# The load of v moved behind the loads of the stored spectrum in SyncE's order

## The chip, the cores and the metric

The kernel runs on one core of one Trainium2 chip. The metric is the device time of one execution in microseconds (us). A profiled execution has a time of its own; the trace of it covers its span, from the first instruction of the program to the last.

## The reference, cut to what matters

A long convolution with gating (batch 4, length 12608, 128 channels), followed by a top-128 selection and a small expert layer:

```python
h_mlp  = np.maximum(pos_emb @ w1, 0.0) @ w2
h_filt = h_mlp * np.exp(-0.01 * pos)[:, None]
u  = x * v
L  = 2 * S
Uf = np.fft.rfft(u, n=L, axis=1)
Hf = np.fft.rfft(h_filt, n=L, axis=0)
y  = np.fft.irfft(Uf * Hf[None, :, :], n=L, axis=1)[:, :S, :]
a  = x * y                                   # the input of the second part
# for each batch: the 128 rows with the highest a @ w_gate
g  = 1.0 / (1.0 + np.exp(-scores[b, top_idx]))
out[b, top_idx] = a[b, top_idx] + g[:, None] * (np.maximum(xe @ w1e, 0.0) @ w2e)
```

## The kernel before

The convolution is done as real transforms of length 93 x 250, written as matmuls. The 128 channels of a batch are 32 groups of four, so there are 4 x 32 = 128 groups, and the main loop takes one group t in each step. All instructions stand on their engines in the order in which the program writes them (a manual schedule); semaphores are set by the framework.

What happens to group t, and where:

- `load_n("x", t)` and `load_n("v", t)` (line 316) bring the inputs, 250 KB each, from DRAM into rings of four (`NU`) and three (`NV`) buffers. Both are issued by SyncE (SP). In step t the loop loads x of group t + 4 and v of group t + 5 (one more in steps 0 to 3, none in step 4).
- `stage_u` (line 326) multiplies x by v on GpSimd (POOL), in step t for group t + 3. It frees a buffer of v.
- `f_s1` (line 484), the first transform on TensorE (PE), reads the product; in step t it is done for group t + 1, and it frees a buffer of x.
- `dft` (line 343), the second transform on PE, then `f_v` and `f_u` on VectorE (DVE, lines 493 and 490).
- `f_y` (lines 500 to 504, DVE) multiplies by the filter's spectrum; in step t it is done for group t - 1. In the first batch the spectrum lies in SBUF (`hh`); the loop stores it to DRAM meanwhile (`hd`, line 1309, 32 stores of 372 KB). From the second batch on `load_h` (line 332) brings it back, two loads of 186 KB a group, into a ring of three buffers. In step t it is issued for group t + 2, whose buffer is the one that `f_y` of group t - 1 has read. The last two batches keep the first three groups, so 178 such loads are issued.
- `f_sd` (lines 511 and 512, POOL), then `f_i` (line 549, PE), the inverse transform, three steps later (`LAG`), with copies on ScalarE (ACT, lines 553 and 554) and `f_c` (line 592, POOL).
- `put` (line 565) moves a part of the result within SBUF, a DMA of 126 KB on SP.

After the last group of a batch (a seam) a stage `P1` of some 40 us computes the product with x, the scores and the output: matmuls of line 639, loads of x (line 614), stores of the output (line 678). The selection of a batch runs in small pieces inside the steps of the next batch.

SP does nothing but issue DMAs, in order: an instruction that waits holds everything behind it. Besides what its data need, each DMA waits for the landing of the one eight places before it, because the framework hands out eight semaphores in turn (`DMAHW0` to `DMAHW7` in the order below).

The lines of the loop that set SP's order in a step:

```python
            if t != 4:
                load_u(t + NU + (t < 4))
...
            for k in range(4 * (t - 1) // 3, min(4 * t // 3, NG)) if t else ():
                nc.sync.dma_start(hd[:, k], hh[:, k].rearrange("p e s i -> p (e s i)"))
            load_h(t + 2)
            for k in due + [k for k in done if k % NG >= NG - 3]:
                put(k, *((JM, NJ) if k % NG >= NG - 3 else ()))
```

Of the kernel before, what the change touches and what calls it, by code (L numbers as in the profile page):

```python
# [39 lines left out]
NU, NV, NX, NH = 4, 3, 5, 3  # L40
# [198 lines left out]
def hyena_moe(ctx, tc, xg, x2, pos, bw, ww, wg, mw1, mw2, cs, c1, gx, cf, ci, wm, tk, out):  # L239
# [18 lines left out]
    def buf(name, k, shape):  # L258
        o, n, w = OFF[name]
        return view(arena, o + k % n * w, shape)  # L260
# [53 lines left out]
    def load_n(n, t):  # L314
        if t < B * NG:
            nc.sync.dma_start(buf(n, t, [NP, XC]), xg[t // NG, :, GC[t], "xv".index(n)])

    def load_u(t, e=1):
        load_n("x", t)
        load_n("v", t + e)  # L320

    def stage_u(t):
        if t >= B * NG:
            return
        x, v = buf("x", t, [NP, XC]), buf("v", t, [NP, XC])
        nc.gpsimd.tensor_tensor(out=x, in0=x, in1=v, op=ALU.mult)  # L326

    def load_h(t):
        if t < B * NG and HS[t] == "hd":
            ht = buf("ht", HI[t], [128, 2, HC])  # L330
            for e in range(2):
                nc.sync.dma_start(ht[:, e], hd[:, GC[t], e * HC:(e + 1) * HC])
# [7 lines left out]
    def dft(t, te, pq):  # L340
        for w in (1, 0):
            for a in range(0, 128, 32):
                nc.tensor.matmul(pq[w][a:a + 32], lhsT=cf_sb[:, 2 * w + a // NQ, a % NQ:a % NQ + 32],  # L343
                                 rhs=te[:, a // NQ], start=True, stop=True)
        qs = buf("qs", t, [128, HC])
        nc.scalar.copy(out=qs, in_=pq[1])  # L346
        return qs
# [130 lines left out]
    def f_s1(t, dst=None, ps=bank1):  # L478
        u = buf("x", t, [NP, 4, N3])
        te = buf("te", t, [128, 2, 4, N1]) if dst is None else dst  # L480
        tps = [view(ps[h], 0, [128, 2, 2, N1]) for h in range(2)]
        for s in range(4):
            for k, c in enumerate(BLK):
                nc.tensor.matmul(tps[s // 2][c, s % 2], lhsT=u[:, s, c], rhs=c1_sb[:, k], start=True, stop=True)  # L484
        for h in range(2):
            nc.scalar.copy(out=te[:, :, 2 * h:2 * h + 2].rearrange("p e s i -> p s e i"), in_=tps[h])  # L486
        return te.rearrange("p e s i -> p e (s i)")

    def f_u(pq, qs):
        nc.vector.tensor_tensor(out=nat(pq[0]), in0=nat(pq[0]), in1=rev(qs), op=ALU.add)  # L490

    def f_v(pq, qs):
        nc.vector.tensor_tensor(out=nat(pq[1]), in0=rev(pq[0]), in1=nat(qs), op=ALU.subtract)  # L493

    def f_y(t, uv):
        ht = buf("ht", HI[t], [128, 2, HC]) if HS[t] != "hh" else hh[:, GC[t]].rearrange("p e s i -> p e (s i)")
        mt, yz = buf("mt", t, [128, 2, HC]), buf("yz", t, [128, 2, HC])
        for e in (1, 0):
            for o, k in ((mt[:, e], 0), (uv[e], 1)):
                nc.vector.tensor_tensor(out=o, in0=uv[e], in1=ht[:, k], op=ALU.mult)  # L500
        yield yz
        nc.vector.tensor_tensor(out=yz[:, 0], in0=uv[1], in1=mt[:, 0], op=ALU.add)  # L502
        yield yz
        nc.vector.tensor_tensor(out=yz[:, 1], in0=mt[:, 1], in1=uv[0], op=ALU.subtract)  # L504
        yield yz
# [56 lines left out]
    def put(t, *cols):  # L562

        o, i = parts(t, cols or (0, NJ))
        nc.sync.dma_start(o, i)

    def turn(i):

        g, r = i % NG, i % 4
        if i > DIR:  # L570
            u = [(t, s) for t in ((i, DIR) if i == DIR + 1 else (i,)) for s in range(4)]
        elif r == 0:
            u = [(i - 1, s) for s in (1, 2, 3)] if g else []
        else:
            u = {1: [(i, 0), (i, 1), (i, 2)], 2: [(i - 1, 3), (i, 0), (i, 1)], 3: [(i - 1, 2), (i - 1, 3), (i, 0)]}[r]
            if g == NG - 1:
                u += [(i, s) for s in (1, 2, 3)]
        done = []
        for t, s in u:
            f_i(t, s)  # L580
            if s == 3:
                done.append(t)
                if t % NG >= NG - 3 and t < DIR:
                    o, i = parts(t, (0, JM))
                    nc.scalar.copy(out=o, in_=i)
        return done

    def f_c(t, ops=(ALU.subtract, ALU.add)):
        a, d = ay[:, GC[t], JM:NJ], ay[:, GC[t], NJ + JM:]
        for op in ops:  # L590
            n = NJ - JM - (op == ALU.add)
            nc.gpsimd.tensor_tensor(out=d if op == ALU.subtract else a[:, :n], in0=a[:, :n], in1=stg(t)[:, :n], op=op)  # L592
# [656 lines left out]
    def small_steps():  # L1249
        for _ in range(ND):  # L1250
            bg.hook("d")

    for t in range(NT + LAG):
        g = t % NG
        i = t - LAG
        bg.now = t
        done = turn(i) if i >= 0 else []
        if t < NT:
            pq = [bank2[2 - 2 * (t % 2) + e] for e in range(2)]
            spare[0] = [a[:, 512 - NS:] for a in bank1]  # L1260
            uv[t] = [a[:, :HC] for a in pq]
            qs = dft(t, te.pop(t), uv[t])
            if t == 0:
                rest()
            bg.hook("p", 2)
            spare[0] = [pq[0][:, HC:]]
            bg.hook("t", 1)
            spare[0] = [a[:, 512 - NS:] for a in bank1]
            bg.hook("n", 1)
            for k in ((1, 2), (3,), (4,), (5,), ())[t] if t < 5 else (t + 1,):  # L1270
                if k < NT:
                    te[k] = f_s1(k, ps=banks[6:] if k == 2 else bank1)
            spare[0] = None
            if t != 4:
                load_u(t + NU + (t < 4))
            if 0 <= t - 4 < len(fills):
                z = fills[t - 4]
                nc.scalar.activation(out=z, in_=one.to_broadcast([128, z.shape[1]]), func=AF.Copy, scale=0.0)
            o = t - 1 in uv
            if o:  # L1280
                steps = f_y(t - 1, uv.pop(t - 1))
                y = next(steps)
                next(steps)
            end = t == NT - 1
            if end:
                next(steps)
            else:
                small_steps()
            f_v(uv[t], qs)
            if o and not end:  # L1290
                next(steps)
            if not end:
                bg.hook("e")
            f_u(uv[t], qs)
            seam = i >= 0 and i % NG == NG - 1
            now = [k for k in done if seam or end or k % NG == NG - 3]
            done_ = [k for k in done if k not in now]
            for k in now:
                f_c(k)
            if o or t - 1 in ys:  # L1300
                sd[t - 1] = f_sd(t - 1, y if o else ys.pop(t - 1))
            for k in done_:
                f_c(k, (ALU.subtract,))
            if not seam and t != 4:
                stage_u(t + 3 + (t < 4))
            for k in done_:
                f_c(k, (ALU.add,))
            for k in range(4 * (t - 1) // 3, min(4 * t // 3, NG)) if t else ():
                nc.sync.dma_start(hd[:, k], hh[:, k].rearrange("p e s i -> p (e s i)"))
            load_h(t + 2)  # L1310
            for k in due + [k for k in done if k % NG >= NG - 3]:
                put(k, *((JM, NJ) if k % NG >= NG - 3 else ()))
            due = [k for k in done if k % NG < NG - 3]
            for _ in range(0 if end else NE):
                bg.hook("e")
            if i >= 0 and i % NG == NG - 1:
                *_, ys[t] = f_y(t, uv.pop(t))
            if t == NT - 1:
                sd[t] = f_last(t, uv.pop(t))
        if t >= NT:  # L1320
            for k in due:
                put(k)
            due = []
            for k in done:
                f_c(k)
        if t == NT:
            bg.drain()
            ex = Experts(picked)
        b = i // NG
        if i >= 0 and i % NG in LA[b]:  # L1330
            if i % NG == LA[b][0]:
                ph[b] = P1(b)
            k, e = divmod(LA[b].index(i % NG), 2)
            ph[b].load_a(AHEAD[k], e * HB, (e + 1) * HB)
        if i % NG == NG - 1 and i >= 0:
            bg.drain("w")
            p1 = ph.pop(b)
            p1.run(ex)
            bg.drain()
            bg = Background(topk_one(b, p1, ex))  # L1340
# [51 lines left out]
```

## Time and profile before

| | |
|---|---|
| time, median of 3 runs | 777.15 us (772.69 to 781.8) |
| the profiled execution's own time | 778.57 us |
| its span in the trace | 776.7 us |
| PE busy (matmuls) | 757.6 us, 98% |
| PEld busy (weight loads) | 554.5 us, 71% |
| DVE, ACT, POOL busy | 684.5, 574.5, 619.7 us |
| DMA, mean over the span | 245 GB/s |

Busy time is the union of an engine's instructions. Idle time of an engine is put down to what ended it: another engine's instruction, a DMA, or "issue", when nothing that the trace shows ended it. A wait of SP is that of its queue (SPq): the time for which its next DMA could not be issued.

### The profile page before, as it was taken

The numbers are of one execution on the slowest core, as the hardware profiler recorded it, in microseconds if no ns is written. First come the engines' busy times: TensorE is split into PE (matmuls) and PEld (weight loads), VectorE is DVE, ScalarE is ACT, GpSimd is POOL, SyncE is SP. The second block draws the span as 40 slices with busy tenths as digits, with TensorE's granted clock in tenths as the row PEclk, the third lists the DMA queues.
The fourth block names the chain that finished last, engine by engine and source line by source line (L and its number), as shares of the span: only waits on it lengthen the run. The fifth ranks groups of instructions, "written<-read, shape, count | busy, mean of one in ns | idle before, by whom it ended". The sixth has DMA issues, their size and how long they took to land. (4 is left out here: it accounts for less than half of the span.)

```text
span 776.7 us, 37673 instructions
## 1 busy us (share of the span) xinstructions
PE 757.6 (98%) x15191; PEld 554.5 (71%) x15191; DVE 684.5 (88%) x1549; ACT 574.5 (74%) x2286; POOL 619.7 (80%) x704
## 2 busy tenths in 40 slices
PE   9999999999999999999999999999999999999996
PEld 9999767887953677777833677889635787786355
DVE  7468699998989899998998998999898999997982
ACT  0324567765669989995779898986699899965892
POOL 0200089999989799999998798999988999998863
PEclk9999999999999999999999999999999999999999
DMA  8200279999899989999689899899789899995880
GB/s 328 89 28 3 62 229 307 298 297 312 226 279 289 326 244 295 284 285 286 193 263 309 281 268 284 260 291 262 205 292 314 266 287 286 286 273 157 251 291 20
DMA packets 95649, 190.44 MB, mean 245 GB/s; under 512 B 11952, under 2 KB 70256, under 8 KB 95472
## 3 DMA queue, kind: packets, MB, share of 16 engines
q1 hardware_dynamic: 95216, 187.48, 79.2%
q8 instruction: 121, 1.98, 1.1%
q0 software_dynamic: 256, 0.52, 0.2%
q14 instruction: 56, 0.46, 0.2%
HBM read 135.34 MB, written 41.35 MB: 227 GB/s over the span
## 5 line engine op out<-in xcount | busy, mean ns | idle before, releaser
L549 PE MATMUL b<-ci_sb,arena 128*31 128x126 f32 x6096 | 202.3, 270 | 5.0 <-issue 4.4
L343 PE MATMUL c<-arena,cf_sb 128*32 128x372 f32 x2032 | 196.1, 477 | 1.5 <-issue 0.6
L484 PE MATMUL a<-c_sb,arena 128*32 128x186 f32 x4064 | 195.2, 321 | 0.9 <-issue 0.8
L326 POOL TENSOR_TENSOR arena<-arena 128x500 f32<-128x500 f32 x128 | 161.6, 1263 | 39.7 <-DMA arena<-in_xg_dram 39.5
L549 PEld LDWEIGHTS b<-ci_sb,arena 128*31 128x31 f32 x6096 | 179.8, 109 | 14.8 <-issue 7.4
L511 POOL TENSOR_TENSOR arena<-arena 128x372 f32<-128x372 f32 x127 | 115.9, 913 | 80.7 <-DVE arena L504 71.8
L486 ACT COPY arena<-a 128x372 f32<-128x372 f32 x252 | 120.3, 477 | 74.2 <-PE a L484 69.2
L484 PEld LDWEIGHTS a<-c_sb,arena 128*32 128x32 f32 x4064 | 142.8, 109 | 37.8 <-issue 14.7
L704 ACT ACTIVATE arena<-arena 128x128 f32<-128x128 f32 x490 | 144.6, 297 | 12.8 <-DVE arena L694 12.4
L553 ACT COPY big<-b 128x412 f32<-128x412 f32 x192 | 109.7, 572 | 14.5 <-PE b L549 12.8
L512 POOL TENSOR_TENSOR arena<-arena 128x372 f32<-128x372 f32 x127 | 115.5, 910 | 0.0
L592 POOL TENSOR_TENSOR big<-big,arena 128x184 f32<-128x184 f32 x194 | 111.7, 577 | 1.3
L343 PEld LDWEIGHTS c<-arena,cf_sb 128*32 128x32 f32 x2032 | 79.4, 109 | 44.7 <-issue 20.7
L500 DVE TENSOR_TENSOR c<-c,arena 128x372 f32<-128x372 f32 x188 | 104.0, 553 | 0.0
L500 DVE TENSOR_TENSOR arena<-c,arena 128x372 f32<-128x372 f32 x188 | 102.3, 544 | 0.0
L704 ACT ACTIVATION_READ_ACCUMULATOR arena<-arena 128x1 f32 x490 | 92.6, 189 | 0.0
L493 DVE TENSOR_TENSOR c<-c,arena 128x372 f32<-128x372 f32 x128 | 71.4, 558 | 20.2 <-ACT arena L346 14.0
L624 POOL TENSOR_TENSOR arena<-big 96x512 f32<-96x512 f32 x64 | 79.3, 1267 | 0.1
L639 PE MATMUL a<-big,gx_sb 96*64 96x512 f32 (+2 forms) x448 | 75.9, 474 | 1.4 <-DVE arena L650 0.8
L490 DVE TENSOR_TENSOR c<-c,arena 128x372 f32<-128x372 f32 x128 | 71.2, 556 | 0.2
L502 DVE TENSOR_TENSOR arena<-c,arena 128x372 f32<-128x372 f32 x127 | 69.7, 549 | 0.0
L346 ACT COPY arena<-c 128x372 f32<-128x372 f32 x128 | 61.4, 480 | 10.8 <-PE c L343 9.8
(218 smaller groups left out, 1087.6 us busy)
## 6 DMA issues: line engine op xcount, KB each, us to landing
arena<-in_xg_dram SPq DMA_DIRECT2D x256, 250.0 KB, 4.7
arena<-hd SPq DMA_DIRECT2D x178, 186.0 KB, 4.9
out_dram<-arena SPq DMA_DIRECT2D x60, 448.0 KB, 5.8
arena<-in_x_dram SPq DMA_DIRECT2D x36, 448.0 KB, 5.0
hd<-big SPq DMA_DIRECT2D x32, 372.0 KB, 5.4
arena<-in_x_dram SPq DMA_DIRECT2D x48, 224.0 KB, 5.3
big<-big SPq DMA_DIRECT2D x84, 126.0 KB, 5.0
big<-in_pos_dram SPq DMA_DIRECT2D x7, 496.0 KB, 6.9
```

Source lines behind the costliest of these rows:

```text
L326: nc.gpsimd.tensor_tensor(out=x, in0=x, in1=v, op=ALU.mult)
L343: nc.tensor.matmul(pq[w][a:a + 32], lhsT=cf_sb[:, 2 * w + a // NQ, a % NQ:a % NQ + 32], rhs=te[:, a // NQ], start=True, stop=True)
L484: nc.tensor.matmul(tps[s // 2][c, s % 2], lhsT=u[:, s, c], rhs=c1_sb[:, k], start=True, stop=True)
L486: nc.scalar.copy(out=te[:, :, 2 * h:2 * h + 2].rearrange("p e s i -> p s e i"), in_=tps[h])
L500: nc.vector.tensor_tensor(out=o, in0=uv[e], in1=ht[:, k], op=ALU.mult)
L511: eng.tensor_tensor(out=nat(sd[:, 0]), in0=nat(yz[:, 0]), in1=rev(yz[:, 1]), op=ALU.add)
L512: eng.tensor_tensor(out=nat(sd[:, 1]), in0=rev(yz[:, 0]), in1=nat(yz[:, 1]), op=ALU.subtract)
L549: nc.tensor.matmul(o3[32 * k:32 * k + NT3, s % 2, e * NJ + js.start:e * NJ + js.stop], lhsT=d[:, e, s, c], rhs=ci_sb[:, e, js], start=True ...
L553: nc.scalar.copy(out=ay[:, GC[t], :NJ + JM, ss], in_=o3[:, :, :NJ + JM].rearrange("p s x -> p x s"))
L592: nc.gpsimd.tensor_tensor(out=d if op == ALU.subtract else a[:, :n], in0=a[:, :n], in1=stg(t)[:, :n], op=op)
L624: nc.gpsimd.tensor_tensor(out=cm[:KP, e].rearrange("p j (g s) -> p j g s", s=4), in0=av[0], in1=av[1], op=op)
L704: nc.scalar.activation(out=x, in_=x, func=AF.Copy, accum_out=self.sc[:, j:j + 1])
```

## The change

The pair `load_u` is split. x of group t + 4 is loaded where it was, early in the step. v of group t + 5 is loaded after the stores of the spectrum and after `load_h`, and before the puts. The instructions of all other engines keep their order and their number; SP has 733 rows before and after.

```diff
             if t != 4:
-                load_u(t + NU + (t < 4))
+                load_n("x", t + NU + (t < 4))
...
             for k in range(4 * (t - 1) // 3, min(4 * t // 3, NG)) if t else ():
                 nc.sync.dma_start(hd[:, k], hh[:, k].rearrange("p e s i -> p (e s i)"))
             load_h(t + 2)
+            if t != 4:
+                load_n("v", t + NU + (t < 4) + 1)
             for k in due + [k for k in done if k % NG >= NG - 3]:
                 put(k, *((JM, NJ) if k % NG >= NG - 3 else ()))
```

SP in a step of the second batch, before. Of the two rows of line 316 the one that waits for PE is x, the one that waits for Pool is v:

```order
L316 DMA arena<-in_xg_dram 128x500 [waits DMAHW4_49,PE_49]
L316 DMA arena<-in_xg_dram 128x500 [waits DMAHW5_49,Pool_49]
L332 DMA arena<-hd 128x372 [waits DMAHW6_49,DVE_49]
L332 DMA arena<-hd 128x372 [waits DMAHW7_49,DVE_49]
L565 DMA big<-big 32x1008 [waits DMAHW0_49,Activation_49,Pool_49]
L614 DMA arena<-in_x_dram 112x512 [waits DMAHW1_49]
```

The same step after:

```order
L316 DMA arena<-in_xg_dram 128x500 [waits DMAHW4_49,PE_49]
L332 DMA arena<-hd 128x372 [waits DMAHW5_49,DVE_49]
L332 DMA arena<-hd 128x372 [waits DMAHW6_49,DVE_49]
L316 DMA arena<-in_xg_dram 128x500 [waits DMAHW7_49,Pool_49]
L565 DMA big<-big 32x1008 [waits DMAHW0_49,Activation_49,Pool_49]
L614 DMA arena<-in_x_dram 112x512 [waits DMAHW1_49]
```

v has moved two places back, the two loads of the spectrum one place forward each; the put and the load of `P1` stay.

SP in two steps of the first batch, before, where the spectrum is stored and not loaded:

```order
L316 DMA arena<-in_xg_dram 128x500 [waits DMAHW4_49,PE_49]
L316 DMA arena<-in_xg_dram 128x500 [waits DMAHW5_49,Pool_49]
L1309 DMA hd<-big 128x744 [waits DMAHW6_49]
L316 DMA arena<-in_xg_dram 128x500 [waits DMAHW7_49,PE_49]
L316 DMA arena<-in_xg_dram 128x500 [waits DMAHW0_49,Pool_49]
L1309 DMA hd<-big 128x744 [waits DMAHW1_49]
L565 DMA big<-big 32x1008 [waits DVE_49,DMAHW2_49,Activation_49,Pool_49]
```

And after:

```order
L316 DMA arena<-in_xg_dram 128x500 [waits DMAHW4_49,PE_49]
L1309 DMA hd<-big 128x744 [waits DMAHW5_49]
L316 DMA arena<-in_xg_dram 128x500 [waits DMAHW6_49,Pool_49]
L316 DMA arena<-in_xg_dram 128x500 [waits DMAHW7_49,PE_49]
L1309 DMA hd<-big 128x744 [waits DMAHW0_49]
L316 DMA arena<-in_xg_dram 128x500 [waits DMAHW1_49,Pool_49]
L565 DMA big<-big 32x1008 [waits DVE_49,DMAHW2_49,Activation_49,Pool_49]
```

Here v has moved behind one store, which waits for no engine.

## Rows read from the trace of the kernel before

**Rows 1.** The page: busy us of each engine, share of the span, instructions.

```profile
PE 757.6 (98%) x15191; PEld 554.5 (71%) x15191; DVE 684.5 (88%) x1549; ACT 574.5 (74%) x2286; POOL 619.7 (80%) x704
```

**Rows 2.** Stretches: start, end, length, busy us by engine, clock, DMA, GB/s.

```profile
97.00:222.00 125.00, 123.17 (x3052) 100.57 (x3044) 118.86 (x259) 83.03 (x207) 119.16 (x142) 1.00 0.90 278
428.00:553.00 125.00, 122.76 (x3112) 100.15 (x3108) 117.12 (x292) 103.56 (x361) 115.35 (x137) 1.00 0.93 269
696.00:777.00 81.00, 70.58 (x892) 43.80 (x891) 56.49 (x145) 51.74 (x275) 54.90 (x65) 0.99 0.58 180
```

**Rows 3.** Waits of PE from 97 to 696 us: total, times, longest.

```profile
PE b L549 <- issue: 4.4, 8, 1.6
PE b L549 <- POOL arena L512: 0.2, 1, 0.2
```

**Rows 4.** Waits of POOL from 97 to 696 us.

```profile
POOL arena L511 <- DVE arena L504: 22.9, 25, 2.3
POOL arena L326 <- DMA arena<-in_xg_dram: 0.5, 1, 0.5
```

**Rows 5.** Timeline of SP in a step of the second batch: start, us, what.

```profile
305.27 1.23 SPq L316 DMA_DIRECT2D arena<-in_xg_dram  x2
306.59 1.06 SPq L332 DMA_DIRECT2D arena<-hd  x2
307.76 0.51 SPq L565 DMA_DIRECT2D big<-big  x1
308.36 2.17 SPq L316 DMA_DIRECT2D arena<-in_xg_dram  x2
```

**Rows 6.** Timeline of POOL around it: stage_u, first and last of four.

```profile
304.88 1.27 POOL L326 TENSOR_TENSOR arena<-arena 128x500 f32<-128x500 f32 x1
...
316.65 1.26 POOL L326 TENSOR_TENSOR arena<-arena 128x500 f32<-128x500 f32 x1
```

**Rows 7.** Timeline of DVE: the last multiplication by the spectrum in that step.

```profile
304.19 0.55 DVE L500 TENSOR_TENSOR c<-c,arena 128x372 f32<-128x372 f32 x1
```

**Rows 8.** Lines 316 and 332: issue time in ns (min/median/max), time to landing.

```profile
L316 SPq DMA_DIRECT2D arena<-in_xg_dram x256: 327/378/1625, 10.4 to 687.6; - x128
...
DMA to landing us min/median/max: 2.6/4.7/7.7
...
L332 SPq DMA_DIRECT2D arena<-hd x178: 320/383/1645, 210.6 to 695.4; - x178
```

**Rows 9.** Waits of SP's queue over the span: total, times, longest.

```profile
SPq L316 <- POOL arena L326: 99.8, 90, 4.7
...
SPq L332 <- DVE arena L500: 20.4, 42, 1.4
```

**Rows 10.** Timeline of SP, then of POOL, after the third seam.

```profile
595.59 2.56 SPq L316 DMA_DIRECT2D arena<-in_xg_dram  x2
598.24 0.98 SPq L332 DMA_DIRECT2D arena<-hd  x2
...
601.91 1.26 POOL L326 TENSOR_TENSOR arena<-arena 128x500 f32<-128x500 f32 x1 [0.51 <-DMA arena<-in_xg_dram]
606.34 1.27 POOL L326 TENSOR_TENSOR arena<-arena 128x500 f32<-128x500 f32 x1
```

**Rows 11.** Four steps of batch one on POOL; stage_u, 428 to 553.

```profile
127.59 1.25 POOL L326 TENSOR_TENSOR arena<-arena 128x500 f32<-128x500 f32 x1
...
142.62 1.25 POOL L326 TENSOR_TENSOR arena<-arena 128x500 f32<-128x500 f32 x1
...
L326 POOL TENSOR_TENSOR arena<-arena 128x500 f32<-128x500 f32 x31 | 39.2, 1265 | 0.0
```

**Rows 12.** The page: DMA queues, packets, MB, share of 16 engines.

```profile
q8 instruction: 121, 1.98, 1.1%
```

## The prediction

> **What bounds the kernel now.** I read the busy times first, then the stretches of the main loop, then who waits for whom, and last the one queue that the change touches. PE is busy for 757.6 of 776.7 us [rows 1]. The 19 us that are left do not lie in the loop. In the first batch (97 to 222 us) PE is idle for 125.00 - 123.17 = 1.83 us, in the third (428 to 553 us) for 125.00 - 122.76 = 2.24 us; the tail after 696 us alone has 81.00 - 70.58 = 10.4 us [rows 2]. The granted clock is 1.00 in both stretches, the upper of the two levels. So the reader is to see a loop with PE at 98 to 99%, and POOL as the next engine, at 115.35 of 125.00 us.
>
> Then the waits in the loop. PE's longest list entry is 4.4 us in 8 waits that no engine and no DMA ended; a wait for POOL has 0.2 us, and none is for a load [rows 3]. POOL, which is the only engine that reads v, waits for DVE (22.9 us); for a load of x or v it waited once in 600 us, for 0.5 us [rows 4]. The change moves loads alone. A load that nobody waits for cannot give time back, so the question is only whether the moved load becomes late, and what its move does to the loads around it.
>
> **The change, part by part.** *Instructions and bytes:* the same number of DMAs on SP, the same bytes, the same order on all other engines. Cost and gain 0.
>
> *The load of v.* Take the step at 305 us. SP issues x and v between 305.27 and 306.50, then the two loads of the spectrum between 306.59 and 307.65, the put at 307.76 and the next x at 308.36 [rows 5]. An issue takes 0.38 us (median) [rows 8], so x is through at 305.65 and v starts at about 306.12. What it waited for in between is the `stage_u` that frees its buffer, which runs from 304.88 to 306.15 [rows 6]. In the new order the two spectrum loads go out at 305.7 and take the 1.06 us that they take now, so they are done at about 306.8, and v, whose buffer has been free since 306.15, follows at 306.8: 0.7 us later than now. Where SP does not wait for POOL, nothing hides them and v is later by the whole 1.15 us from 306.50 to 307.65.
>
> *What hides that.* v goes into a ring of three, so the product that needs it is three `stage_u` further on, at 316.65 [rows 6]. From 306.12 to 316.65 are 10.5 us. A load of line 316 lands after 4.7 us (median), 7.7 us at the slowest [rows 8]. The spare is 5.8 us, or 2.8 us for the slowest landing. A shift of 0.7 to 1.15 us fits into both, so on the path it costs 0. The lower bound is the same 0: v is not waited for now, hence earlier or later makes no gain.
>
> *A new wait in front of v.* The spectrum loads wait for DVE's multiplications of group t - 1. The last of these ends at 304.19 + 0.55 = 304.74 [rows 7], 0.95 us ahead of the earliest moment at which SP could now issue them. Line 332 does show waits for DVE, 42 with 20.4 us, the longest 1.4 us [rows 9]. Put fully on top, v is late by 1.15 + 1.4 = 2.55 us, still inside the 2.8 us. I take 0, and keep this as the point where the cover ends. Behind v stand the put and, a place later, the next x.
>
> *The loads of the spectrum* go out earlier, by the wait for POOL that now stands in front of them: 99.8 us in 90 waits, 1.1 us on average, the longest 4.7 [rows 9]. Nobody waited for them before, so the gain is 0. Seen from SP, this wait is mostly overlapped instead of standing between issues.
>
> *The load of x* is the tight one: POOL's 0.5 us of waiting is for it, after the third seam, where x was issued at 595.59 and the product started at 601.91 [rows 10]. Between two loads of x SP issues the same DMAs in both orders. Where POOL was waited for, the next x comes earlier, by up to the 0.5 us of our step; where DVE holds the spectrum loads, v comes behind that wait instead of ahead of it, and x is later by one issue, 0.38 us. Either is a part of a wait that POOL can absorb: it has 125.00 - 115.35 = 9.65 us of idle time in 31 steps [rows 2, 11], 0.31 us a step. Taken: 0.
>
> *After a seam* v is tightest. The second load of the pair from 595.59 to 598.15 is v; its product runs at 606.34 [rows 10]. 606.34 - 597.8 = 8.5 us, less 4.7 us leaves 3.8; the two spectrum loads take 0.98 us there, so 2.8 us stay. At the slowest landing it would be late by 0.2 us, at three seams 0.6 us of POOL, and PE did not wait for a loss of 0.51 us there. Taken: 0.
>
> *In the first batch* v passes a store of the spectrum (or two). The store waits for no engine by then, and costs an issue or two. Taken: 0.
>
> *PE's own waits.* The 4.4 us in [rows 3] are of a kind that loads could touch: the program's instructions come by DMA too. They are 121 packets with 1.1% of 16 engines' span [rows 12], 0.011 x 16 x 776.7 / 121 = 1.13 us each, on engines that are 0.90 to 0.93 busy [rows 2]. If a denser row of loads delays them, the 4.4 us may double; if a smoother one helps, they may vanish. I take 0 of it with 4.4 us to both sides. The Trainium skill (DMA: Bandwidth & Descriptors, Queues, rings and completion order) says that a DMA engine takes turns between its queues, a packet each; by that rule the order within SP's queue would leave these 4.4 us alone. No run here shows it yet.
>
> Sum: 0 us on the profiled execution's 778.57 us. That one stood 1.4 us above the median of the three runs, 777.15 us, and the forecast is for the median: 777 us. The three runs lie within 772.69 and 781.8 us, so about 1%, or 7.8 us, is what a measurement can tell from no change.
>
> **The rivals.** *Faster, hidden stalls.* Idle time of PE may hide within its busy time. Four steps of the first batch take 142.62 - 127.59 = 15.03 us, 3.76 us each; from 428 to 553 us 31 steps take 4.03 us each [rows 2, 11]. The 0.27 us of difference, over the three batches that load the spectrum (31 steps each), are 25 us. A part of it is the selection's own work in these steps. If half is stalls that come from late loads, and these go, the time is 777 - 12 = 765 us. Against it: no engine that feeds PE is seen to wait for a load [rows 4]; for it: it is just in the batches with spectrum loads that the pace is lower. The Trainium skill (Perfetto Trace Analysis, Identifying the Most-Contended Engine) says that matmul busy time is not a good measure of how near the limit PE is, and that the share of weight loads is; that share is 71% [rows 1], so by that rule there is room. The trace speaks for the loads as its cause in nothing.
>
> *Slower, v late.* The place is `stage_u` on POOL in the 178 / 2 = 89 steps with spectrum loads [rows 8]. If the chain "DVE frees the spectrum's buffer, two issues, v" shifts v by more than 2.8 us where landings are slow, POOL stands, takes up 0.31 us a step out of its idle time and hands the rest to PE through `f_sd`. Each 0.1 us beyond that costs 8.9 us; 0.15 us make 777 + 13 = 790 us. It decides from a shift of 3.1 us in most steps. Against it: the bound of 2.55 us above, and the median landing, with which it would take 6.1 us.
>
> *The change does nothing.* If SP always reached v after `stage_u` was done, the spectrum loads gain nothing and v is 1.15 us later: 777 us too. The 90 waits [rows 9] speak against that in most steps, and the time is the same.
>
> **How the numbers follow.** No change, by the sum or by the last rival, 0.81, between 772 and 782 us (4.4 us to both sides of 777, rounded out). Hidden stalls 0.09, around 765 us. v late 0.07, around 790 us. The 0.03 that are left are for a measured median that strays by over 1% by itself, 0.01 down and 0.02 up. So faster by over 1% 0.10, within 1% 0.81, slower by over 1% 0.09. The range should leave out no more than 0.2. From 768 to 785 us it holds the first case with its spread, and a part of the two others where only a third of the hidden stalls goes, or v is late at few places.
>
> **What the profile of the changed kernel would show.** PE busy again near 757 us, and 1 to 3 us of idle time in the same two stretches. SP's wait of line 316 for POOL falls from 99.8 us to well under half, since spectrum loads go out during it; waits of line 332 for DVE grow. In a step at about 305 us v starts 0.5 to 1.2 us after the `stage_u` that frees its buffer, where it now starts at once. POOL's waits for line 316 stay at the start and, at most, after seams. If POOL's `stage_u` shows waits for a load in the middle of the second to fourth batch, the cover of v was smaller than I worked out and the prediction is wrong on the slow side. If PE's busy time falls by more than 5 us with the same matmuls, stalls were hidden in it, and I am wrong on the fast side.

## The result, and the profile after

The changed kernel takes 781.59 us (median of 22 runs, 775.05 to 783.95), the kernel before on the same chip 777.2 us (22 runs): a ratio of 1.0053, 95% interval 1.0032 to 1.0074. It is slower by 2.5 to 5.8 us. That is less than the 1% up to which the forecast spoke of no change, and yet more than the runs scatter by chance. Two further timings of the same kernel are told below; all three together give 2.7 us, within 0.9 (0.35%; "within" stands for the half of a 95% interval). Differences of means, here and below, leave out the few executions that took over 1.5% more than the fastest of the same kernel.

The page of the profiled execution (span 782.1 us, 5.4 us longer than before) has nearly the same busy times (PE 757.6 us before); what grew is the time in which PE stands, 5.0 us in front of line 549 before and 10.0 now:

```profile
PE 757.1 (97%) x15191; PEld 558.7 (71%) x15191; DVE 685.1 (88%) x1549; ACT 572.9 (73%) x2286; POOL 620.0 (79%) x704
...
q8 instruction: 121, 1.98, 1.1%
...
L549 PE MATMUL b<-ci_sb,arena 128*31 128x126 f32 x6096 | 204.0, 270 | 10.0 <-issue 9.2
```

The stretches that answer to [rows 2] (start, end, length, busy us by engine, clock, DMA share, GB/s):

```profile
97.00:222.00 125.00, 120.16 (x2964) 98.92 (x2959) 117.00 (x256) 79.56 (x199) 115.61 (x138) 1.00 0.89 271
428.00:553.00 125.00, 122.25 (x3080) 98.34 (x3080) 117.00 (x292) 103.80 (x374) 115.33 (x136) 1.00 0.91 271
696.00:777.00 81.00, 76.09 (x1048) 49.35 (x1038) 62.67 (x159) 55.22 (x286) 60.57 (x72) 1.00 0.62 194
```

In the first batch PE now does 3.0 us less in the same 125 us, in the third 0.5 us less, and what is missing stands in the tail. The granted clock is the same, 1.00 in both. The waits of PE from 97 to 696 us answer to [rows 3], those of POOL to [rows 4]:

```profile
PE b L549 <- issue: 9.2, 12, 1.7
PE a L484 <- DVE arena L650: 1.0, 1, 1.0
PE a L484 <- issue: 0.8, 1, 0.8
PE c L343 <- DVE arena L502: 0.6, 1, 0.6
PE c L343 <- issue: 0.6, 1, 0.6
```

```profile
POOL arena L511 <- DVE arena L504: 30.6, 33, 2.2
POOL arena L694 <- DVE arena L650: 6.1, 4, 1.9
```

PE's waits on line 549 that no engine and no semaphore ended went from 4.4 us in 8 to 9.2 us in 12. POOL has no wait for a load of x or v at all between 97 and 696 us. So in this execution the loads that were moved are not late; PE is, for another reason.

SP in the step at 305 us, which answers to [rows 5] (start, duration, what), and POOL's `stage_u` beside it, as in [rows 6]. The loop is 3.65 us later by then, so the first `stage_u` here belongs to the step before that of [rows 6]; the second, at 308.53, is the one that ran at 304.88 before:

```profile
303.87 1.27 SPq L316 DMA_DIRECT2D arena<-in_xg_dram  x1
305.24 0.86 SPq L332 DMA_DIRECT2D arena<-hd  x2
306.23 0.36 SPq L316 DMA_DIRECT2D arena<-in_xg_dram  x1
306.63 0.42 SPq L614 DMA_DIRECT2D arena<-in_x_dram  x1
307.34 0.33 SPq L316 DMA_DIRECT2D arena<-in_xg_dram  x1
```

```profile
304.93 1.27 POOL L326 TENSOR_TENSOR arena<-arena 128x500 f32<-128x500 f32 x1
308.53 1.25 POOL L326 TENSOR_TENSOR arena<-arena 128x500 f32<-128x500 f32 x1
```

x goes out at 303.87, the two spectrum loads behind it while `stage_u` still runs, and v at 306.23, 0.03 us after that product ends (304.93 + 1.27 = 306.20). The order did what it says: v starts as soon as its buffer is free, as before, and the spectrum loads go out ahead of it. SP's waits over the span, which answer to [rows 9], and the time to landing of lines 316 and 332 ([rows 8]):

```profile
SPq L316 <- POOL arena L326: 85.0, 77, 3.8
...
SPq L332 <- DVE arena L500: 18.2, 25, 3.2
```

```profile
L316 SPq DMA_DIRECT2D arena<-in_xg_dram x256: 327/381/1732, 9.7 to 693.1; - x128
...
DMA to landing us min/median/max: 2.7/4.9/8.3
```

What PE waits for can be read from two views beside each other. The timeline of PE around the stall at 156.5 us:

```profile
150.96 0.42 PE L549 MATMUL b<-ci_sb,arena 128*31 128x126 f32 x7
151.67 1.34 PE L549 MATMUL b<-ci_sb,arena 128*31 128x126 f32 x41 [0.30 <-issue]
...
155.28 1.25 PE L549 MATMUL b<-ci_sb,arena 128*31 128x126 f32 x38
157.51 0.51 PE L549 MATMUL b<-ci_sb,arena 128*31 128x126 f32 x9 [0.98 <-issue]
```

PE stops in the middle of a product: 7 matmuls, a gap, 41 more of the same line and tiles; a step later 38, a gap of 0.98 us, 9 more. An operand that came late would be expected to hold up the first matmul of a product, not the eighth or the thirty-ninth, and to show a semaphore. The view of the DMA queues for 155.05 to 156.02 us shows what came in just before:

```profile
DMA packets 128, 0.27 MB, mean 279 GB/s; under 512 B 13, under 2 KB 102, under 8 KB 127
...
q1 hardware_dynamic: 127, 0.25, 78.2%
q8 instruction: 1, 0.02, 6.0%
```

One packet of the instruction queue, 16 KB. Between 67 and 83 us of the trace before, where few loads run, these packets start exactly 256 of PE's instructions apart, so I take them to be PE's. Single records of the trace put it at 155.08 to 156.00, and PE goes on at 157.51, 1.51 us after it has landed. So it is at nearly every stall of over 0.2 us between 97 and 696 us: 14 of 17 in the changed kernel (10.5 of 12.3 us) and 10 of 12 before (5.2 of 6.1 us) end 1.25 to 1.75 us after such a packet has landed. Packets come every 6 us, so by chance one in twelve would. PE waits for its own instructions, and in this execution of the changed kernel it does so for twice as long as in that of the kernel before.

### The profile page after: what moved, and what is told of

It reads as the page before. It is cut to its first block, busy times and chain, and to the rows that moved or that the text cites. A ratio compares the mean times of both kernels' runs of the same rounds, so it can differ in the third digit from the quotient of the medians.

```text
span 782.1 us, 37673 instructions
## 1 busy us (share of the span) xinstructions
PE 757.1 (97%) x15191; PEld 558.7 (71%) x15191; DVE 685.1 (88%) x1549; ACT 572.9 (73%) x2286; POOL 620.0 (79%) x704
## 5 line engine op out<-in xcount | busy, mean ns | idle before, releaser
L549 PEld LDWEIGHTS b<-ci_sb,arena 128*31 128x31 f32 x6096 | 182.0, 109 | 20.1 <-issue 11.9
L484 PEld LDWEIGHTS a<-c_sb,arena 128*32 128x32 f32 x4064 | 145.4, 109 | 37.7 <-issue 12.9
L343 PEld LDWEIGHTS c<-arena,cf_sb 128*32 128x32 f32 x2032 | 81.9, 109 | 41.2 <-issue 16.6
L500 DVE TENSOR_TENSOR c<-c,arena 128x372 f32<-128x372 f32 x188 | 102.1, 543 | 0.0
L500 DVE TENSOR_TENSOR arena<-c,arena 128x372 f32<-128x372 f32 x188 | 100.3, 534 | 0.0
L493 DVE TENSOR_TENSOR c<-c,arena 128x372 f32<-128x372 f32 x128 | 70.3, 549 | 24.5 <-ACT arena L346 14.8
L490 DVE TENSOR_TENSOR c<-c,arena 128x372 f32<-128x372 f32 x128 | 69.9, 546 | 0.2
L502 DVE TENSOR_TENSOR arena<-c,arena 128x372 f32<-128x372 f32 x127 | 67.7, 533 | 0.0
```

Of the source, the lines that this page charges most:

```text
L549: nc.tensor.matmul(o3[32 * k:32 * k + NT3, s % 2, e * NJ + js.start:e * NJ + js.stop], lhsT=d[:, e, s, c], rhs=ci_sb[:, e, js], start=True ...
```

## The experiments

Each run stands beside the kernel before on the same chip. Four theories: **A**, the new order of SP's DMAs delays PE's instruction packets on the DMA engines; **B**, v lands late and POOL hands that on; **C**, the difference is chance; **D**, the order costs by itself, whatever the bytes.

**The place.** v at its new place in the first batch alone (`e1_first`; `e1_later` has the two conditions the other way round):

```diff
-                load_u(t + NU + (t < 4))
+                load_n("x", t + NU + (t < 4))
+                if not t < NG:
+                    load_n("v", t + NU + (t < 4) + 1)
...
+            if t != 4 and t < NG:
+                load_n("v", t + NU + (t < 4) + 1)
```

> v stands behind the stores of the spectrum in the first batch only (steps before 32); from the second batch on it stands where it stood before. Theory A (PE stands for its own instructions: their packets come late behind loads that SP now issues in a denser row, because the wait for stage_u no longer stands between them): a part of the loss, about 1 to 3 us over before (ratio 1.001 to 1.004), and PE's waits ended by issue longer in the first batch only. Theory B (v itself comes late after the seams and in the steps with spectrum loads): 0, ratio 1.000, since no spectrum is loaded in these steps. Theory C (the difference is chance): 1.000.

> v stands behind the loads of the spectrum from the second batch on only. Theory A: the other part of the loss, 1 to 3 us over before (ratio 1.001 to 1.004). Theory B: the whole loss, 4 us (1.005), with waits of POOL for loads or of PE after the three seams. Theory C: 1.000.

Measured: first batch alone 778.83 against 776.13 us, 1.0045 (1.0014 to 1.0076); later batches alone 776.0 us, 0.9999 (0.997 to 1.0027). That speaks against B: there v is tightest, and nothing is lost here (a second timing, below, gave 0.24%). POOL's waits for loads of x and v from 97 to 696 us, 0.3 and 1.4 us in the two executions of that kernel and 0.7 at most in the changed one, speak against it more plainly. The first seemed to say that the loss lies in the first batch; this did not hold (below).

**The wait apart from the bytes.** v in two pieces, its first 32 of 500 columns at the old place and the rest at the new one (`e1_gate`), or both pieces at the old place (`e1_split`):

```diff
+                load_n("v", t + NU + (t < 4) + 1, 0, 32)
...
+            if t != 4:
+                load_n("v", t + NU + (t < 4) + 1, 32)
```

> v in two pieces: its first 32 columns (16 KB) at the old place, where SP waits for stage_u as before, the other 468 columns behind the loads of the spectrum. One more DMA a step. Theory A: the wait is back between x and the spectrum loads, so the time is that of the split load at the old place, within 1.5 us, and under the changed kernel. Theory B: most of v is as late as in the changed kernel, so the time is at or above the changed kernel's, 4 to 6 us over before.

> The control for the piece-wise load: both pieces of v one behind the other at the old place. Theories A and B both: before's time plus what one more DMA a step costs, 0 to 3 us (ratio 1.000 to 1.004).

Measured: 782.31 us, 1.0086 (1.0056 to 1.0116), and 783.11 us, 1.0086 (1.0052 to 1.012). The split costs 7 us in either order, against the 0 to 3 us that I expected: one DMA more in a step, and rows of 128 bytes in its first piece. So the pair doesn't tell where the wait may stand. The cause is another one than in the changed kernel, as the waits of POOL from 97 to 696 us show, first with the piece moved, then with both in place:

```profile
POOL arena L327 <- DMA arena<-in_xg_dram: 9.9, 11, 2.0
```

```profile
POOL arena L327 <- DMA arena<-in_xg_dram: 7.9, 14, 1.0
```

This is what a late load looks like in the waits; the changed kernel has none of it in two executions and 0.7 us in a third. Between the two orders nothing differs here, and PE's waits for instructions are 1.5 and 2.1 us in the whole span.

**Fewer bytes.** Both orders, with x and v of groups 8 to 95 loaded by half their columns (the products go on with what stood in the buffers, so the later result differs; every instruction stays):

```diff
-            nc.sync.dma_start(buf(n, t, [NP, XC]), xg[t // NG, :, GC[t], "xv".index(n)])
+            s = 2 if 8 <= t < 3 * NG else 4
+            nc.sync.dma_start(buf(n, t, [NP, s * N3]), xg[t // NG, :, GC[t], "xv".index(n), :s])
```

> The old order, with x and v loaded to the half only (two of the four channels of a group) from group 8 to group 95, so the first three batches compute with stale data; all instructions stay. Theory A (PE stands because its instruction packets come late behind the loads in the DMA engines): waits of PE that issue ended fall from 5 us to under 2 us in the loop, time 10 to 18 us under before (ratio 0.977 to 0.987). Theory D (the loss is a wait of SP or of another engine that follows from the order of the stores alone, not from bytes): time within 4 us of before.

> The changed order with the same half loads (the first three batches compute with stale data). Theory A: within 1.5 us of the old order with half loads, since there is nothing left to wait behind; the 4 us of the change are gone. Theory D: still 3.5 to 4.5 us over the old order with half loads.

Measured: old order 770.55 us, 0.9907 (0.988 to 0.9933); new order 769.73 us, 0.9913 (0.9887 to 0.9938). Both gain 7 us, less than the 10 to 18 that I expected of theory A, and the new order loses nothing against the old one that shows (means -0.2 us, within 1.8). PE's waits from 97 to 696 us, old order, then new (a line of code more stands ahead, so line 550 is line 549 of before):

```profile
PE b L550 <- issue: 3.5, 5, 1.2
PE a L485 <- issue: 0.8, 2, 0.5
```

```profile
PE b L550 <- issue: 1.5, 3, 0.6
PE a L485 <- issue: 0.6, 1, 0.6
```

The busy times of PE and PEld, old order, then new, with all matmuls still there:

```profile
PE 753.5 (98%) x15191; PEld 556.3 (72%) x15191; DVE 684.5 (89%) x1549; ACT 572.8 (74%) x2286; POOL 619.4 (80%) x704
```

```profile
PE 752.6 (98%) x15191; PEld 548.7 (71%) x15191; DVE 683.9 (89%) x1549; ACT 572.8 (75%) x2286; POOL 619.5 (81%) x704
```

PE's busy time is 4.1 us under that of the kernel before in the old order and 4.5 us under that of the changed kernel in the new one; ten executions with all bytes have 754.9 to 757.9 us. So a part of the gain is time that the profile had counted as busy. The waits of the old order stayed at 4.3 us in all, where I had expected under 2. On the orders the pair says this: with fewer bytes the new order's loss is 2.9 us smaller, within 2.0. So D falls, if narrowly, and A fits: where the DMA engines carry less, the order doesn't matter. The pair alone would fit any other delay that grows with the bytes of the loads as well.

**Fewer instructions.** Both orders, the products of line 343 with 64 columns of weights in place of 32, 14167 matmuls in place of 15191:

```diff
-            for a in range(0, 128, 32):
+            for a in range(0, 128, NQ):
```

> The old order with the second transform in matmuls of 64 columns of weights instead of 32: half as many matmuls and weight loads on that line, some 16 of 192 instructions of PE in a step. Bytes of loads and all other engines stay. Theory A: PE asks for a packet of instructions every 5.5 us instead of every 5.1 us, so fewer are late: 4 to 10 us under before (ratio 0.987 to 0.995). Theory D: no change but that of the matmuls themselves, within 2 us.

> The changed order with the same wide matmuls. Theory A: under the changed kernel by 4 to 10 us, and within 2.5 us of the old order with wide matmuls: the difference of the change shrinks. Theory D: 3.5 to 4.5 us over the old order with wide matmuls.

Measured: 794.85 us, 1.0238 (1.0209 to 1.0267), and 795.81 us, 1.0244 (1.0217 to 1.027). The wider matmuls are slower by themselves (PE 780.8 us busy), which says nothing on the question; but PE's waits for instructions shrink to 0.9 and 0.2 us in the span, and the two orders are alike (means +0.3 us, within 1.7). As this pace is lower, it leaves every load more time too, so it speaks for A, but not for A alone.

**Which of the moved DMAs.** The changed kernel again (`e3_after_again`); the old order with the stores of the spectrum behind the put (`e3_hdlast`); both orders with each put a step later:

```diff
-            for k in due + [k for k in done if k % NG >= NG - 3]:
+            for k in due2 + [k for k in done if k % NG >= NG - 3]:
...
-            due = [k for k in done if k % NG < NG - 3]
+            due, due2 = [k for k in done if k % NG < NG - 3], due
```

> The changed kernel once more, as the measure for the other three: 3 to 5 us over before (ratio 1.004 to 1.006). All theories agree.

> The old order, but the stores of the spectrum stand behind the put instead of between v and the put; only the first batch differs. Theory A1 (in the changed kernel x overtakes the stores, which then stand last in the row, right in front of the next wait for stage_u): here the store still stands in front of x, so the time is before's, within 1.5 us (ratio 0.998 to 1.002). Theory A2 (in the changed kernel the put follows v at once, SP waits there for POOL, and what stands behind it goes out in a denser row): the put follows v here too, so 2 to 4.5 us over before (1.003 to 1.006).

> The changed order, with each put one step later, so that SP need not wait for POOL in front of it. Theory A1: the loss stays, 3 to 5 us over the same edit on the old order. Theory A2: the loss is gone, within 1.5 us of the same edit on the old order.

> The control: the old order with each put one step later. Theories A1 and A2: within 1.5 us of before, since the store stands between v and the put there and hides SP's wait for POOL.

Measured: changed again 778.78 us, 1.0018 (0.9989 to 1.0047); stores last 776.54 us, 0.9992 (0.996 to 1.0024); late puts 784.66 us, 1.009 (1.0062 to 1.0119), in the new order, and 784.06 us, 1.0073 (1.0047 to 1.0099), in the old one. The repeat was smaller than the first timing. A store that stands last costs nothing by itself. A put right behind v, as the stores last have it in the old order, costs nothing either. Late puts cost 6 to 7 us by themselves (PE then waits for them at the seams, 4.5 us in the old order and 2.2 in the new one), which leaves the pair without a clear answer.

Four more kernels followed. Two have the two orders with stores of the spectrum that carry half of their bytes (the other half is filled ahead of the loop by 32 stores more, from a table, so the later result differs); `e4_xphv` has the order x, put, store, v in the first batch; `e4_first_again` is `e1_first` once more.

```diff
-                nc.sync.dma_start(hd[:, k], hh[:, k].rearrange("p e s i -> p (e s i)"))
+                nc.sync.dma_start(hd[:, k, :HC], hh[:, k, 0].rearrange("p s i -> p (s i)"))
```

> The order of before; each store of the spectrum in the first batch carries only half of its bytes (the other half of the buffer is filled once, ahead of the loop, with a table of another step, so the later batches compute with a wrong spectrum there). If the first batch loses because stores stand between the loads and PE's instruction packets, fewer bytes cost nothing or gain: 774 to 778 us, PE's issue waits from 97 to 222 us 0 to 1 us. If bytes of the stores play no part, the same as before within 1 us, and the changed order beside it stays 3 us above it.

> The changed order with the same halved stores (the other half of the buffer filled ahead of the loop with a table of another step, so the later batches compute with a wrong spectrum there). If the bytes of the stores that the order puts behind x and v make PE's packets late, the difference to its partner with the order of before shrinks from about 3 us to 1.5 us or less. If the order itself does it, whatever the stores carry, the difference stays 3 us or more.

> In the first batch SP issues x, put, store, v in a step, from the second batch on the order of before. Between two waits for POOL this is v, x, put, store: as in the changed kernel x stands ahead of the store, and the store is last, but the put no longer stands directly behind v. If the loss comes from x overtaking the store, 2 to 4 us over before, 779 to 781 us. If it comes from the put directly behind v, 0 to 1 us over before.

> Once more the kernel in which v stands at its new place in the first batch alone. It stood 0.45% above before (0.14 to 0.76%), the whole change once 0.53% and once 0.18%. If the first batch carries the loss, 0.2 to 0.6% above before, 779 to 782 us; if that was chance, within 0.15%.

Measured: half stores, old order, 773.53 us, 0.9953 (0.9929 to 0.9978); new order 775.25 us, 0.9972 (0.995 to 0.9993): means 2.6 us apart, within 1.9. Stores with half of their bytes save 4 us in the old order, so their bytes in the loop are a part of what holds PE up, but the difference of the orders does not need them.

Order x, put, store, v: 779.31 us, 1.0021 (0.9991 to 1.0051), means +2.5 us, within 1.6. The expectation says that this kernel has the order of before from the second batch on; its code has the order of the changed kernel there, as a step of its trace shows, x first, then the spectrum, then v:

```profile
303.62 0.53 SPq L316 DMA_DIRECT2D arena<-in_xg_dram  x1
304.25 0.86 SPq L332 DMA_DIRECT2D arena<-hd  x2
305.21 0.38 SPq L316 DMA_DIRECT2D arena<-in_xg_dram  x1
```

So it is the changed kernel with another order in the first batch, and as slow as that. It tells neither whether the put behind v costs nor whether x ahead of the store does. First batch again: 778.0 us, 0.9999 (0.9979 to 1.0019). With that my reading of the first timing fell.

**The place once more.** The changed kernel a third time, beside `e1_later` a second time:

> The changed kernel a third time, beside the kernel in which v is moved from the second batch on. If the order makes PE's packets late, 0.2 to 0.5% above before (779 to 781 us), and the profiled execution lies on the line that the traces so far give, 773.4 us with about 5 us of PE's issue waits, 782.1 us with 10.8. If the loss was chance, within 0.15% of before.

> v at its new place from the second batch on, a second time. If the loss comes from the first batch, within 0.15% of before again, and 2 us or more below the changed kernel beside it. If it comes from the loop as a whole, half to three quarters of the changed kernel's loss is here, 0.15 to 0.4%.

Measured: changed 779.95 against 774.79 us, 1.0073 (1.0045 to 1.01); later batches alone 777.27 us, 1.0024 (0.9999 to 1.0049). PE's waits over the span, the changed kernel, then the other:

```profile
PE b L549 <- issue: 4.9, 11, 1.0
...
PE a L484 <- issue: 1.7, 3, 0.9
...
PE c L343 <- issue: 0.7, 3, 0.3
```

```profile
PE b L549 <- issue: 2.5, 5, 1.0
...
PE a L484 <- issue: 0.2, 1, 0.2
...
PE c L343 <- issue: 0.2, 1, 0.2
```

All timings of one kernel taken together (differences of the means, weighted by their variances): the whole change +2.7 us, within 0.9; in the first batch alone +1.1, within 1.1; from the second batch on alone +1.0, within 1.2. Neither part is clear of zero by itself, and their sum, 2.1 within 1.6, agrees with the whole. The whole is clear of zero, so C falls. The loss is spread over the loop, or at least no batch was shown to carry it.

The ten profiled executions of the six kernels that have all bytes, all matmuls and no added or delayed DMA tell more. The second column is all of PE's time without a releaser over the span. The third is how long after PE's request a packet of instructions starts: nine of ten packets between 97 and 696 us are no later than this (the request is set at 170 instructions of the 256 before, about where packets start in the stretches without loads).

| kernel | span us | PE's issue waits us | packet starts late by us |
|---|---|---|---|
| before | 776.7 | 6.0 | 3.79 |
| changed | 782.1 | 10.8 | 4.01 |
| changed, again | 777.1 | 8.5 | 3.95 |
| changed, third | 778.2 | 7.5 | 3.85 |
| first batch alone | 773.4 | 5.4 | 3.70 |
| first batch alone, again | 775.3 | 6.4 | 3.42 |
| later batches alone | 773.4 | 4.6 | 3.44 |
| later batches alone, again | 770.6 | 3.1 | 3.38 |
| x, put, store, v (later batches as changed) | 778.1 | 7.7 | 3.52 |
| stores last | 779.2 | 8.8 | 3.57 |

Span and waits rise together, by 1.43 us of span for each us of waits, with a correlation of 0.96 over the ten. So the waits for instructions go with most of what one execution differs from another by. That they also carry the mean difference of the orders fits, but is not shown by this table: the kernel before has one row, 1.6 us above that line; the second execution of the changed kernel lies 1.6 below it; and the stores last, which are no slower in the mean, have 8.8 us of waits in a long execution. The three executions of the changed kernel have the latest packets, by 0.06 to 0.22 us over before.

## Why the prediction was wrong, point by point

- **PE's own waits: this step failed.** It named the cause, instruction packets on busy DMA engines, and its bound ("may double"), and then took 0 between +4.4 and -4.4 us. The list entry went from 4.4 to 9.2 us in the first execution; over the span all such entries went from 6.0 to 10.8, 8.5 and 7.5 us in three. By 1.43 us for each us their mean, 8.9, gives 4.2 us, an estimate from one execution of the kernel before; the timings gave 2.7, within 0.9. So the term was there, its sign was plus, and the 0 was wrong by about that much. I had the traffic and the packets in view, and no row that told the sign; 0 was the middle of the bounds, not a reading.
- **The page I weighed against it.** The packets do start late, by 2.4 us on average in the loop before. The Trainium skill (DMA: Bandwidth & Descriptors, Queues, rings and completion order) puts a packet at 9 to 17 descriptors typically and at most 64, and says that an engine drains one before it turns to the next queue. In the trace before, the rows of SP's DMAs take 0.102 us each on average from 97 to 696 us, so 2.4 us are 24 of them, between the page's typical packet and its largest. The longest lateness there, 5.2 us, is 51, but one packet in the trace with the stores last is 7.4 us late, 73 of them. By this count the average fits the rule and the longest does not in every trace; no trace shows which rows a packet waited behind. What I drew from it was wrong. The rule speaks of how long one instruction packet waits behind another queue; it does not say that the order of the DMAs leaves that wait alone.
- **The load of v, and the wait of line 332 in front of it: right, 0.** No wait of POOL for a load of x or v from 97 to 696 us (0.7 us in two in the third execution), though single waits for DVE reached 3.2 us instead of 1.4 and the slowest landing 8.3 instead of 7.7 us. v starts 0.03 us after its buffer is free at 305 us, not the 0.5 to 1.2 us of the signs: the spectrum loads fit under the wait.
- **The loads of the spectrum earlier: right, 0.** SP's wait of line 316 for POOL fell only from 99.8 to 85.0 us, not well under half: the wait is as long, it just has two issues fewer behind it.
- **x, and v after a seam: right, 0.** The tight x lost its 0.5 us of waiting in the first execution.
- **The first batch: 0 taken.** Not refuted: 1.1 us, within 1.1.
- **Rivals.** v late: not so. That the change does nothing: not so. Hidden stalls: they exist, but the order does not free them. Fewer bytes of x and v did: the time fell by 7 us, and PE's busy time by 4.1 and 4.5 us with the same matmuls (5.8 with half stores in the old order), about the 5 us that the prediction named as the sign. So that rival had the loads right. Whether the hidden part is PE waiting for its instructions or for something else, no run shows.
- **What stays open.** Why just this order should make more packets late. The bytes of the stores don't explain it (2.6 us are left with half of them), and neither does a put right behind v (stores last: -0.5 us, within 1.8). x ahead of the stores, or of the spectrum loads, was not tested by itself. The mean lateness of the packets differs little (2.45 us before; 2.60, 2.37 and 2.43 changed); if the packets do the harm, it is the long ones.

## What to carry to other kernels

Where the DMA engines are 90% busy and PE is the bound, as here, PE's instructions are a load like any other, and the one that nobody schedules: look for waits without a releaser in the middle of a run of equal matmuls, and for a packet of the instruction queue that landed 1.3 to 1.7 us ahead of their end. A reordering of DMAs whose data nobody waits for can then still cost, and fewer bytes can gain where no load is late. Time a change of half a per cent more than once: the same kernel gave +0.18, +0.53 and +0.73%.

## What the runs showed of the hardware

- A 16 KB packet of instructions takes 1.15 us in the loop (a row of SP's DMAs: 0.102 us on average), and PE goes on about 1.45 us after it has landed.
- The span of an execution goes with its instruction stalls: 3.1 us of them at a span of 770.6 us, 10.8 at 782.1, correlation 0.96 over ten executions.
- Products of line 343 with 64 columns of weights take 489 ns each where those with 32 take 477, half as many, and the kernel still became 18 us longer.
- With half of the bytes of x and v PE was busy for 753.5 and 752.6 us, with the same 15191 matmuls; ten executions with all bytes have 754.9 to 757.9.
- v in two DMAs a step, 32 and 468 columns, of the same bytes in all, cost 7 us, and showed as POOL waiting for loads, 8 to 10 us.
